# One order table for five engines, exchanged for another: masks, copies and products placed anew in an attention and gated-unit kernel

## The chip, the cores and the metric

The kernel runs on one core of one Trainium2 chip. The metric is the device time of one execution in microseconds (us), the median of several runs. The engines are TensorE (PE, with its weight loads PEld), VectorE (DVE), ScalarE (ACT), GpSimd (POOL) and SyncE (SP), which here only issues DMAs.

## What is computed

Eight batches of 576 rows, eight heads of 64. Attention with a causal mask and a decay from a running sum of `s`; its output `x` goes into a gated linear unit whose gate is a causal convolution of five taps over the rows.

```python
scores = (q @ k.T) / 8 + minimum(cum[k] - cum[q], 0)   # cum = cumsum(max(s, 0)); later keys are masked
x      = softmax(scores) @ v                           # heads side by side: 8 x 576 x 512
gate   = sigmoid(sum(conv_w[j] * x shifted by 4 - j))  # five taps, per column
out    = (gate * (x @ w_val)) @ w_out
```

## The kernel before

The unit of work is a pair of heads of one batch, numbered `n = 4 * batch + pair`, 0 to 31. Its attention gives 128 columns of `x`, and the gated unit then works on those columns, so the same `n` is also a column block of the second half.

**One pair, step by step.** `s0`, `s1`, `s2` are score products on TensorE into two PSUM banks each (L505); `e0`, `e1`, `e2` take their exponentials on ScalarE, 128x1024 elements each, into a buffer `P` (L556; three buffers in turn). The last 64 queries of all four pairs of a batch have their own step, `s4` and `e4` (L532). In `s0` lie the four diagonal blocks, which need the causal mask. It is made in one of two ways: TensorE adds a product of two constant tiles `fut` to the scores, very negative above the diagonal (L518, two products of 512 columns), or GpSimd sets the upper part of `P` to zero after the exponential (`mk`, `AFFINE_SELECT`, L579). The kernel takes the second way for the pairs that have an `mk` step in the table. `av0` and `av` multiply `P` with `Vp` (L594), where `Vp` is `v` times the decay weight, made on GpSimd (`vp`, L474, one instruction per pair). `rec` and `nm` (L607, L613, VectorE) divide by the row sum into `xn`; `xt` turns it (L626, TensorE, into a bank) and `xe` copies the bank to `xT` (L373).

**The gate.** `t1` to `t4` add the four shifted taps into `gp`. On VectorE a tap is one instruction that reads the bank (L665, L670). On GpSimd it is two: `p2`, `p3` or `p4` makes the product `pr` from `xT` (L654), and `t` adds it (L673). ScalarE can make `pr` too (L652). `th` is the tanh (L690), `val` the product with `w_val` (L703), `glu` joins them (L712), `out` is the product with `w_out` (L723), `oe` copies its bank into `ot` (L373), `st` stores it.

**Loads.** Of batches 1 to 7, `q` and `k` come in as fp32 (`ld_q`, `ld_k`), are cast (`c_q`, `c_k`), turned on TensorE (`qq`, L629) and copied into `QKT` (`qe`). `ld_t`, `tt` and `te` do the same for the last 64 rows, `ld_v` loads `v` into `vst`. Nearly all loads and all stores are issued by SyncE, in the order of the table.

**What sets the order.** A table, `ORDER`, a string of 1157 steps. A step is `name.numbers:engine:slots`: `vp.1.0:G` is the decay weighting for pair 0 of batch 1 on GpSimd, `e0.5:A` the first exponential of pair 5 on ScalarE, `s0.4:T:6+7:0` a product into PSUM banks 6 and 7 whose exponentials go into `P` buffer 0. Letters are S (SyncE), G (GpSimd), T (TensorE), A (ScalarE), V (VectorE). The program walks the table once and calls each step's function; every engine gets its instructions in that order, and a framework adds the waits. The last four pairs (batch 7) are cut into rows 0 to 383 and 384 to 575: `u0` to `u3`, `f0` to `f3`, `ml` and steps that end in `.0` or `.1`. `wu` (L620) are products of the identity with itself whose result nobody reads.

Of the kernel before, what the change touches and what calls it, by code (L numbers as in the profile page):

```python
# [197 lines left out]
centre:V s0.1:T:4+5:1 ld_k.1.0:S:2 s2.1:T:2+3 e0.1:A qt.0.2.q:T:1 c_k.0.2:V decT:T:0 ld_cw:S e2.0:A qt.0.2.k:T:4
mk.1:G wu.20:T:5 ld_k.1.1:S qe.0.2.k:V wu.21:T:5 wu.22:T:5 qe.0.2.q:A s1.1:T:6+7 c_k.0.3:V e2.1:A s0.2:T:4+5:2
c_q.0.3:G ld_v.0.2:S expw:A qt.0.3.q:T:1 e1.1:A s4.0.1:T:2+3 qe.0.3.q:V vp.0.0:G qt.0.3.k:T:0 qe.0.3.k:V e4.0.1:A  # L200
ld_q.1.0:S:3 e0.2:A s2.2:T:6+7 s1.2:T:2+3 vp.0.1:G av0.0:T:0+1 e2.2:A av.0:T ld_v.0.3:S mk.2:G rec.0:V av0.1:T:4+5
e1.2:A nm.0:V av.1:T c_k.1.0:G:2 s0.3:T:6+7:0 rec.1:V s2.3:T:2+3 e0.3:A nm.1:V ld_t.1:S cwT:T:0 xt.0:T:1 c_k.1.1:G
cwc:V xt.1:T:4 e2.3:A wu.23:T:6 xe.0:V ld_q.1.1:S vp.0.2:G qq.1.1:T:0:7 t1.0:V:0 s4.0.2:T:2+3 s1.3:T:5+6 e4.0.2:A
xe.1:V c_q.1.0:A:0 s4.0.3:T:2+3 mk.3:G t3.0:V ld_v.1.2:S e4.0.3:A t1.1:V:1 e1.3:A ld_v.1.1:S av0.2:T:2+3 vp.0.3:G
av.2:T t2.0:V ld_v.1.0:S qe.1.3:A tt.1:T:5 ld_v.1.3:S qe.1.2:V p4.1:G:0 p4.0:A:1 ld_v.1.4:S ld_wv:S:4 av0.3:T:6+7
av.3:T te.1:A rec.2:V ld_t.2:S t4.1:G c_q.1.1:G nm.2:V s0.6:T:0+1:1 rec.3:V xt.2:T:5 nm.3:V e0.6:A t4.0:G s0.7:T:2+3:2
xe.2:V s2.6:T:6+7 e0.7:A qq.1.0:T:0:1 t1.2:V:2 mk.6:G p2.1:A:0 s1.6:T:2+3 t3.2:V qe.1.0:A ld_q.2:S:0 mk.7:G qe.1.1:V
e2.6:A t3.1:V s1.4:T:0+1 e1.6:A s0.4:T:6+7:0 t2.2:V ld_k.2:S:1 xt.3:T:4 e0.4:A s0.5:T:2+3:0 t2.1:G t4.2:V s2.4:T:6+7
xe.3:V wu.24:T:5 e2.4:A vp.1.0:G mk.4:G wu.25:T:5 t1.3:V:3 wu.26:T:5 wu.27:T:5 ld_wo:S:2 wu.28:T:5 e1.4:A s4.1.3:T:6+7
ld_t.3:S t3.3:V wu.29:T:5 wu.30:T:5 e4.1.3:A s1.5:T:0+1 t4.3:V wu.31:T:5 th.2:A:0 ld_q.3:S:3 vp.1.2:G av0.4:T:6+7  # L210
th.1:A:1 av.4:T t2.3:V e0.5:A vp.1.1:G cast_wv:G rec.4:V av0.6:T:4+5 nm.4:V av.6:T e1.5:A s2.5:T:2+3 rec.6:V
s1.7:T:6+7 nm.6:V e2.5:A xt.4:T:0 ld_v.2.2:S c_q.2:G:1 tt.2:T:1 xe.4:V th.0:A:2 av0.5:T:2+3 t1.4:V:2 av.5:T te.2:A
ld_v.2.4:S val.3.0:T:4 th.3:A:3 p4.4:G:1 rec.5:V val.3.1:T:1 nm.5:V e1.7:A val.1.0:T:5 glu.3.0:V t4.4:G xt.5:T:2
c_k.2:A:2 glu.3.1:V ld_v.2.1:S val.1.1:T:3 glu.1.0:V s2.7:T:6+7 glu.1.1:V qq.2.0:T:1:5 vp.1.3:G xe.5:V val.0.0:T:3
t2.4:V e2.7:A val.0.1:T:4 t1.5:V:1 p2.5:G:0 qe.2.0:A av0.7:T:6+7 glu.0.0:V glu.0.1:V ld_v.2.3:S val.2.0:T:3 t2.5:G
p3.5:A:1 t3.4:V av.7:T ld_v.2.0:S qe.2.1:A qq.2.1:T:4:2 ld_k.5:S:4 rec.7:V cast_wo:G nm.7:V val.2.1:T:0 qe.2.3:A
xt.6:T:5 glu.2.0:V xt.7:T:1 xe.6:V qe.2.2:A s0.9:T:6+7:1 glu.2.1:V s1.9:T:2+3 p4.5:G:0 xe.7:V out.0.2:T:0 e0.9:A
t1.6:V:0 out.0.0:T:4 t3.5:G t1.7:V:3 e1.9:A ld_k.3:S:0 t4.6:V s1.8:T:6+7 oe.0.2:A:0 s0.8:T:2+3:0 mk.9:G oe.0.0:A:1
t3.7:V val.7.0:T:0 e0.8:A ld_t.4:S out.0.3:T:4 t2.6:V p3.6:G:1 e1.8:A t2.7:V out.0.1:T:2 t3.6:G th.4:A:4 t4.7:V
val.4.0:T:3 st.0.2:S val.7.1:T:7 glu.4.0:V th.7:A:3 val.4.1:T:1 t4.5:G oe.0.3:V:2 th.6:A:1 ld_v.3.2:S s2.8:T:5+6  # L220
glu.7.1:V s4.2.3:T:3+4 glu.7.0:V e2.8:A val.6.0:T:7 glu.4.1:V vp.2.0:G val.6.1:T:0 glu.6.0:V e4.2.3:A ld_v.3.3:S
oe.0.1:V:3 s0.10:T:5+6:2 th.5:A:2 c_q.3:G:0 s2.9:T:3+4 glu.6.1:V av0.8:T:1+2 e2.9:A av.8:T val.5.0:T:0 ld_q.5:S:1
e0.10:A rec.8:V nm.8:V vp.2.1:G s2.10:T:3+4 val.5.1:T:7 e2.10:A glu.5.0:V s1.10:T:1+2 glu.5.1:V s0.11:T:5+6:0 vp.2.2:G
e1.10:A xt.8:T:0 av0.9:T:3+4 xe.8:V tt.3:T:7 e0.11:A p4.8:G:1 t1.8:V:2 av.9:T ld_t.5:S qq.3.0:T:1:2 te.3:A rec.9:V
c_k.3:G:1 nm.9:V s1.11:T:5+6 qe.3.1:A out.0.7:T:7 ld_v.3.4:S t2.8:V qe.3.0:A av0.10:T:3+4 st.0.1:S oe.0.7:V:4 xt.9:T:0
t4.8:G av.10:T e1.11:A xe.9:V ld_v.3.0:S s0.12:T:1+2:1 rec.10:V t1.9:V:3 out.0.6:T:7 e0.12:A vp.2.3:G nm.10:V
ld_v.3.1:S s1.12:T:5+6 oe.0.6:A:5 s2.11:T:1+2 t3.9:V xt.10:T:3 e1.12:A p3.8:G:0 out.0.8:T:7 xe.10:V e2.11:A t4.9:V
ld_q.4:S:2 mk.11:G s2.12:T:5+6 oe.0.8:V:0 e2.12:A qq.3.1:T:4:1 t3.8:G t1.10:V:0 tt.4:T:7 qe.3.3:A av0.11:T:5+6 t2.10:V
st.0.6:S av.11:T p3.10:G:1 qe.3.2:A ld_k.4:S:3 out.0.4:T:1 rec.11:V t4.10:V te.4:A c_q.5:G:2 nm.11:V s0.14:T:3+4:2
st.0.3:S out.0.5:T:7 e0.14:A oe.0.4:V:3 t2.9:V s4.3.3:T:5+6 th.8:A:0 ld_v.4.2:S t3.10:G xt.11:T:4 e4.3.3:A  # L230
s0.13:T:2+3:0 xe.11:V s2.13:T:0+1 e0.13:A ld_v.4.1:S val.8.0:T:5 t1.11:V:1 vp.3.3:G val.10.0:T:6 th.10:A:3 glu.8.0:V
s1.13:T:2+3 t3.11:V vp.3.1:G val.8.1:T:5 e2.13:A st.0.4:S glu.10.0:V t2.11:V e1.13:A val.10.1:T:6 mk.13:G val.9.0:T:0
glu.8.1:V oe.0.5:A:5 ld_k.6:S:0 glu.10.1:V val.9.1:T:1 mk.14:G t4.11:V th.9:A:4 s2.14:T:2+3 qq.5.0:T:7:6 e2.14:A
glu.9.0:V c_k.5:G:0 av0.13:T:4+5 qe.5.0:V av.13:T qe.5.1:A val.11.0:T:0 ld_v.4.4:S rec.13:V glu.9.1:V th.11:A:1
s1.14:T:2+3 s0.15:T:6+7:0 nm.13:V vp.3.2:G e1.14:A val.11.1:T:1 glu.11.0:V xt.13:T:4 ld_v.4.0:S glu.11.1:V e0.15:A
mk.12:G s1.15:T:2+3 xe.13:V s2.15:T:0+1 st.0.5:S t1.13:V:2 e2.15:A qq.5.1:T:7:6 c_q.4:G:1 out.1.1:T:5 t2.13:V qe.5.2:A
qe.5.3:V av0.14:T:0+1 e1.15:A c_k.4:G:2 av.14:T out.1.2:T:7 rec.14:V p4.13:A:0 nm.14:V oe.1.1:A:2 qq.4.0:T:6:2
# [602 lines left out]
```

## Time and profile before

| | |
|---|---|
| median of 3 runs (lowest, highest) | 188.84 us (188.75, 188.96) |
| span of the profiled execution, first to last instruction | 187.6 us |
| busy share: PE, DVE, ACT, POOL | 91%, 87%, 91%, 88% |
| instructions: PE, DVE, ACT, POOL | 2704, 321, 230, 149 |
| HBM read and written | 30.57 MB, 9.44 MB |

No time of the profiled execution is listed beside its span; the median of the runs lies 1.24 us above it. A row of a view by groups reads: line, engine, operation, output <- input with shapes, count | busy us, mean ns of one | idle us of the engine ahead of it and what ended that. A row of the timeline starts with start and length in us. In the table by windows each engine has its busy us and its count. A busy TensorE is not TensorE at its peak, since the ends of products are modelled.

### The profile page before, as it was taken

The numbers are of one execution on the slowest core, as the hardware profiler recorded it, in microseconds if no ns is written. First come the engines' busy times: TensorE is split into PE (matmuls) and PEld (weight loads), VectorE is DVE, ScalarE is ACT, GpSimd is POOL, SyncE is SP. The second block draws the span as 40 slices with busy tenths as digits, with TensorE's granted clock in tenths as the row PEclk, the third lists the DMA queues.
The fourth block names the chain that finished last, engine by engine and source line by source line (L and its number), as shares of the span: only waits on it lengthen the run. The fifth ranks groups of instructions, "written<-read, shape, count | busy, mean of one in ns | idle before, by whom it ended". The sixth has DMA issues, their size and how long they took to land.

```text
span 187.6 us, 6637 instructions
## 1 busy us (share of the span) xinstructions
PE 170.1 (91%) x2704; PEld 113.5 (60%) x2720; DVE 163.3 (87%) x321; ACT 170.6 (91%) x230; POOL 164.5 (88%) x149
## 2 busy tenths in 40 slices
PE   6898885888899998998978999999999999999991
PEld 2556573476757765576745667586566865776560
DVE  4355999878997899999999899998989899999980
ACT  2589899899999999999999999999999999999772
POOL 5267999899999999999978999999999989899610
PEclk9999999999999999999999999999999999999999
DMA  5998999999999999999298999899541003401164
GB/s 164 274 277 246 231 225 243 343 388 341 193 232 304 277 303 258 389 270 283 71 248 184 274 333 325 193 314 247 164 162 66 3 0 115 171 3 56 61 224 175
DMA packets 62283, 40.46 MB, mean 216 GB/s; under 512 B 47333, under 2 KB 49381, under 8 KB 62250
## 3 DMA queue, kind: packets, MB, share of 16 engines
q1 hardware_dynamic: 61706, 39.49, 77.1%
q8 instruction: 22, 0.36, 0.8%
q10 hardware_dynamic: 544, 0.52, 0.8%
q14 instruction: 11, 0.09, 0.2%
HBM read 30.57 MB, written 9.44 MB: 213 GB/s over the span
## 4 chain that ended last, share of the span: by engine, by line
PE 50%; ACT 15%; SPq 9%; DMA 8%; issue 6%; POOL 5%; DVE 4%; ACTq 0%; POOLq 0%; DVEq 0%
PE bank L723 14%; PE bank L703 11%; PE bank L594 10%; ACT P L556 9%; PE bank L505 7%; DMA vst<-in_v_dram 6%; SPq L435 3%; PE bank L629 3%; PE bank L626 3%; POOL gp L673 2%; DMA first<-in_k_dram 2%; ACT th L690 2%; SPq L471 2%; ACT QKT L373 2%; SPq L467 2%
## 5 line engine op out<-in xcount | busy, mean ns | idle before, releaser
L556 ACT ACTIVATE P<-bank 128x1024 bf16<-128x1024 f32 x84 | 82.9, 1042 | 4.1 <-PE bank L505 3.0
L670 DVE SCALAR_TENSOR_TENSOR gp<-bank,cwr,gp 128x574 f32<-128x574 bf16 (+6 forms) x72 | 52.3, 740 | 0.9 <-POOL gp L673 0.5
L673 POOL TENSOR_TENSOR gp<-gp,pr 128x572 f32<-128x572 f32 (+6 forms) x36 | 45.1, 1259 | 4.4 <-DVE gp L670 1.7
L474 POOL TENSOR_TENSOR Vp<-vst,w 128x650 bf16<-128x650 f32 x32 | 40.7, 1288 | 2.8 <-DMA vst<-in_v_dram 1.8
L505 PE MATMUL bank<-QKT 64*128 64x128 bf16 (+4 forms) x592 | 37.2, 237 | 4.8 <-ACT P L556 1.8
L703 PE MATMUL bank<-xT,wv 128*128 128x288 bf16 (+2 forms) x256 | 38.5, 287 | 1.1 <-ACT P L556 0.5
L594 PE MATMUL bank<-Vp,P 128*128 128x65 bf16 x960 | 36.0, 194 | 2.4 <-POOL Vp L474 1.1
L594 PEld LDWEIGHTS <-P 128*128 128x128 bf16 x960 | 33.2, 97 | 6.8 <-issue 1.5
L723 PE MATMUL bank<-wo,glu 128*128 128x512 bf16 x128 | 34.1, 380 | 1.5 <-issue 0.5
L505 PEld LDWEIGHTS <-QKT 64*128 64x128 bf16 x592 | 19.4, 94 | 22.3 <-issue 14.6
L712 DVE SCALAR_TENSOR_TENSOR glu<-th,bank 128x288 bf16<-128x288 f32 (+2 forms) x64 | 27.5, 445 | 2.0 <-ACT th L690 0.9
L703 PEld LDWEIGHTS <-wv 128*128 128x128 bf16 x256 | 22.4, 97 | 11.0 <-issue 4.8
L654 POOL TENSOR_TENSOR pr<-xT,cwr 128x572 f32<-128x572 bf16 (+6 forms) x28 | 28.3, 1020 | 0.6 <-ACT xT L373 0.6
L373 ACT COPY QKT<-bank 128x1024 bf16<-128x1024 bf16 (+1 forms) x26 | 24.2, 966 | 3.8 <-PE bank L489 2.9
L613 DVE TENSOR_TENSOR xn<-bank,recs 128x640 bf16<-128x640 f32 (+2 forms) x36 | 26.8, 745 | 0.6
L665 DVE SCALAR_TENSOR_TENSOR gp<-xT,cwr,bank 128x576 f32<-128x576 bf16 (+2 forms) x36 | 26.4, 741 | 0.7
L579 POOL TENSOR_SCALAR_AFFINE_SELECT P<-P 128x1024 bf16<-128x1024 bf16 (+1 forms) x22 | 22.3, 1021 | 4.2 <-ACT P L556 4.2
L690 ACT ACTIVATE th<-gp,cwr 128x576 f32<-128x576 f32 x28 | 22.0, 794 | 0.1
L723 PEld LDWEIGHTS <-glu 128*128 128x128 bf16 x144 | 12.4, 98 | 13.2 <-issue 1.6
L373 ACT COPY ot<-bank 128x512 f32<-128x512 f32 x26 | 15.2, 610 | 1.5 <-PE bank L723 1.0
L626 PE MATMUL bank<-ident,xn 128*128 128x128 bf16 x164 | 14.9, 219 | 0.7 <-ACT P L556 0.3
L373 POOL CAST qkb<-qkf 128x2048 bf16<-128x2048 f32 (+1 forms) x9 | 14.4, 1619 | 0.0
(66 smaller groups left out, 174.8 us busy)
## 6 DMA issues: line engine op xcount, KB each, us to landing
out_dram<-ot SPq DMA_DIRECT2D x36, 256.0 KB, 4.3
vst<-in_v_dram SPq DMA_DIRECT2D x28, 256.0 KB, 5.9
first<-in_q_dram SPq DMA_DIRECT2D x6, 512.0 KB, 6.0
first<-in_k_dram SPq DMA_DIRECT2D x6, 512.0 KB, 6.2
qkf<-in_q_dram SPq DMA_DIRECT2D x6, 512.0 KB, 6.7
qkf<-in_k_dram SPq DMA_DIRECT2D x6, 512.0 KB, 7.3
vst<-in_v_dram SPq DMA_DIRECT2D x15, 128.0 KB, 5.4
first<-in_q_dram SPq DMA_DIRECT2D x4, 256.0 KB, 5.3
```

The costliest lines, as they stand in the source:

```text
L373: (act.copy if e is act else e.tensor_copy)(dst, src)
L474: e.tensor_tensor(Vps[b % 2][:, :, HP[p]], vslot(b)[:, :, HP[p]], w[:, :, b * 8 + 2 * p:b * 8 + 2 * p + 2].unsqueeze(3).to_broadcast([128, ...
L505: pe.matmul(ps[:, hh, c0:c0 + nq], QKTs[b % 2][r, 1, p, k0:k0 + 128], QKTs[b % 2][r, 0, p, q0:q0 + nq], **kw)
L556: act.activation(out=Pt(n)[:, :, step * 512:(step + 1) * 512], in_=pair((f"s{step}", n)), func=AF.Exp, scale=0.125)
L594: pe.matmul(ps[:, o:o + 65], lhsT, Vps[b % 2][:, kb, 2 * p + w, :], start=(kb == 0), stop=(kb == qb))
L613: vec.tensor_tensor(xns[b % 2][:, g, p * 128:(p + 1) * 128].rearrange("t g (w d) -> t w g d", w=2), ps[:, :, :, 0:64], recs[:, n, :, g].un ...
L654: pool.tensor_tensor(pr, xTs[b % 2][:, c, 4 + lo - m:4 + hi - m], r.to_broadcast([128, hi - lo]), ALU.mult)
L670: vec.scalar_tensor_tensor(gp[:, lo:hi], xps(n, *h)[:, lo - m:hi - m], r, gp[:, lo:hi], ALU.mult, ALU.add)
L673: pool.tensor_tensor(gp[:, lo:hi], gp[:, lo:hi], prs[at[f"p{m}", n, *h][0]][:, lo:hi], ALU.add)
L703: pe.matmul(ps, wv[:, dc, c * 128:(c + 1) * 128], xTs[b % 2][:, dc, 4 + lo:4 + hi], start=(dc == 0), stop=(dc == 3))
L712: vec.scalar_tensor_tensor(glu2[:, c, o + lo:o + hi], th[:, lo:hi], 1.0, ps, ALU.add, ALU.mult)
L723: pe.matmul(bank_of(u, i), glu2[:, c, i * 128:i * 128 + 128], wo[:, c, :], start=(c == 0), stop=(c == 3))
```

## The change

`ORDER` is replaced as a whole: 1119 steps in place of 1157, in another sequence, with other engines for some steps and other banks and buffers. By kind of step, before and after:

- masks on GpSimd: `mk` 18 to 2 (pairs 11 and 25), `ml` 4 to 1; the other masks become products with `fut` on TensorE: 32 more of 512 columns and 6 of 128
- `wu` 32 to 10
- tap products `pr`: ScalarE 8 to 0, GpSimd 28 to 39; taps added on GpSimd 36 to 39, on VectorE 72 to 69
- copies into `QKT` (`qe`): ScalarE 26 to 23, VectorE 10 to 13; copies out of the last product (`oe`): ScalarE 26 to 28, VectorE 10 to 8; copies into `xT` (`xe`): ScalarE 12 to 13, VectorE 24 to 23
- casts of `q` and `k`: ScalarE 3 to 1, VectorE 4 to 3, GpSimd 17 to 20
- the number of every other step, and what it computes, stays

Two lines of the table, the start of it before and after, and the edits outside it:

```diff
-ld_k.0.0:A ld_q.0.0:S ld_k.0.1:A wu.0:T:0 ld_t.0:S wu.1:T:7 wu.2:T:0 wu.3:T:7 ld_s:S wu.4:T:0 ld_q.0.1:S wu.5:T:7
+ld_k.0.1:A ld_k.0.0:A ld_q.0.0:S ld_t.0:S ld_s:S ld_q.0.1:S ld_cw:S ld_q.0.2:S c_k.0.0:V ld_k.0.2:S c_q.0.0:V wu.0:T:7
...
-    Pt = lambda n, h=None: Ps[at["s0" if h is None else f"u{2 * h}", n][1]]
+    split = lambda n: n in splits
+
+    def Pt(n, h=None):
+        steps = ("e0", "e1", "e2") if h is None else (f"f{2 * h}", f"f{2 * h + 1}")
+        return Ps[next(at[f, n] for f in steps if (f, n) in at)[0]]
...
-            split = ("u0", n) in at
-            g = ((3, 1)[h] if split else 4)
-            d = Pt(n, h if split else None)[:, :, 0:128 * g].rearrange("k w (g q) -> k w g q", g=g)
+            g = ((3, 1)[h] if split(n) else 4)
+            d = Pt(n, h if split(n) else None)[:, :, 0:128 * g].rearrange("k w (g q) -> k w g q", g=g)
...
-        two = at["val", n, 0][0]
-        j = two[hf] if isinstance(two, list) else at["val", n, hf][0]
+        j = at["val", n, hf][0]
...
+    splits = {int(name.split(".")[1]) for name, *_ in steps if name.startswith("u0.")}
```

The edits outside the table let the `P` buffer be named on the exponential step (`e0.5:A:0`) and let the three exponentials of a pair come in any order.

**GpSimd around the first `Vp` of batch 1.** These are its rows before, `P` being the buffers of exponentials, `pr` and `gp` tap products and sums, `vst` the loaded `v`:

```order
L654 TENSOR_TENSOR pr_134<-xT_113,cwr 128x572
L673 TENSOR_TENSOR gp_120<-gp_120,pr_134 128x572
L373 CAST qkb_102<-qkf_137 128x2x8x64
L673 TENSOR_TENSOR gp_119<-gp_119,pr_135 128x572
L579 AFFINE_SELECT P_117<-P_117 128x2x512
L579 AFFINE_SELECT P_118<-P_118 128x2x512
L673 TENSOR_TENSOR gp_120<-gp_120,pr_134 128x574
L474 TENSOR_TENSOR Vp_110<-vst_93,w 128x5x130
L579 AFFINE_SELECT P_116<-P_116 128x2x512
L474 TENSOR_TENSOR Vp_110<-vst_93,w 128x5x130 x2
L373 CAST wv<-qkf_138 128x2048
```

The same place on GpSimd in the changed kernel, with the same names:

```order
L657 TENSOR_TENSOR pr_135<-xT_113,cwr 128x574
L373 CAST qkb_103<-qkf_137 128x2x8x64 x2
L676 TENSOR_TENSOR gp_120<-gp_120,pr_134 128x573
L657 TENSOR_TENSOR pr_134<-xT_113,cwr 128x572
L676 TENSOR_TENSOR gp_119<-gp_119,pr_134 128x572
L474 TENSOR_TENSOR Vp_110<-vst_93,w 128x5x130 x3
L676 TENSOR_TENSOR gp_120<-gp_120,pr_135 128x574
L373 CAST wv<-qkf_138 128x2048
```

The two masks ahead of the first `Vp` of batch 1 and the one right behind it are gone, and three `Vp` stand in a row.

**ScalarE about a batch later.** These are its rows before, where the four copies into `QKT` of batch 2 stand; `qkb` is the cast `q` and `k`, `ot` the buffers that are stored:

```order
L373 CAST qkb_104<-first 128x4x8x64
L556 ACTIVATE P_118<-bank 128x2x512
L373 COPY QKT_107<-bank 128x2x2x256
L652 ACTIVATE pr_135<-bank,cwr 128x573
L373 COPY QKT_107<-bank 128x2x2x256 x3
L556 ACTIVATE P_117<-bank 128x2x512 x2
L373 COPY ot_128<-bank 128x512
```

The same copies on ScalarE in the changed kernel, `th` being the tanh and `xT` the turned output of the attention:

```order
L691 ACTIVATE th_125<-gp_119,cwr 128x576
L691 ACTIVATE th_126<-gp_122,cwr 128x576
L373 COPY xT_114<-bank 128x576
L373 COPY QKT_107<-bank 128x2x2x256 x2
L373 COPY xT_114<-bank 128x576 x2
L560 ACTIVATE P_118<-bank 128x2x512
L373 COPY QKT_107<-bank 128x2x2x256
```

The cast and the tap product `pr` have left ScalarE here, one of the four copies into `QKT` has gone to VectorE, and three copies into `xT` have come.

More of the change, by code (lines that the diff above doesn't have):

```diff
@@ L198 @@
[L198 to L237, printed above, removed]
@@ L294 @@
+oe.3.5:V:0 out.3.7:T outa.3.8:T:0 oe.3.7:V:4 st.3.5:S out.3.8:T chk:V st.3.7:S oe.3.8:A:2 cnt:T:7 cntc:V st.3.8:S
+flag:S
 """
@@ L674, in tap @@
         return f
-    split = lambda n: ("u0", n) in at
     def thof(n):
```

160 lines of the change are left out of this document (99 added, 61 removed).

## The prediction

> **What bounds the kernel now.** I read the busy line of the page first, then the table by windows, then the timelines at the places where the windows change character.
>
> ```profile
> PE 170.1 (91%) x2704; PEld 113.5 (60%) x2720; DVE 163.3 (87%) x321; ACT 170.6 (91%) x230; POOL 164.5 (88%) x149
> 0.00:37.81 37.81, 30.74 (x459) 18.79 (x460) 27.27 (x53) 29.84 (x41) 28.49 (x36) 1.00 0.98 251
> 37.81:175.08 137.27, 130.95 (x2176) 89.74 (x2191) 129.00 (x244) 134.14 (x176) 133.42 (x109) 1.00 0.77 212
> 175.08:182.12 7.04, 6.99 (x66) 4.46 (x65) 6.43 (x21) 5.47 (x14) 2.58 (x6) 1.00 0.37 136
> ```
>
> Four engines are within eight us of each other, so none bounds the whole; the windows (busy us of PE, PEld, DVE, ACT, POOL, then clock, DMA share and GB/s) show three stages. Until 37.81 us every engine idles for 7 to 10.5 us while the DMA share is 0.98: the loads bound. From there to 182.12, where the last `glu` ends, lie 144.31 us: ScalarE is busy for 134.14 + 5.47 = 139.61 of them and waits 4.70; TensorE 137.94, GpSimd 136.00, VectorE 135.43. ScalarE is the tightest, and all are tight.
>
> Where the first stage ends is seen in one row each of GpSimd (two), TensorE and VectorE:
>
> ```profile
> 34.23 1.28 POOL L474 TENSOR_TENSOR Vp<-vst,w 128x650 bf16<-128x650 f32 x1 [0.90 <-DMA vst<-in_v_dram]
> 35.46 1.10 POOL L579 TENSOR_SCALAR_AFFINE_SELECT P<-P 128x1024 bf16<-128x1024 bf16 x1
> 36.61 1.09 PE L594 MATMUL bank<-Vp,P 128*128 128x65 bf16 x30 [0.22 <-POOL P L579]
> 37.81 0.22 DVE L607 RECIPROCAL recs<-bank 128x10 f32<-128x10 f32 x1 [0.72 <-PE bank L594]
> ```
>
> `vp.1.0` waits for the load of `v` of batch 1; then comes a mask, then `av0.4` and `av.4`, then `rec.4`. All of batch 1 passes through here. The end:
>
> ```profile
> 178.97 0.59 POOL L673 TENSOR_TENSOR gp<-gp,pr 128x192 f32<-128x192 f32 x1 [0.46 <-DVE gp L670]
> 181.15 0.46 ACT L684 ACTIVATE th<-gp,cwr 128x192 f32<-128x192 f32 x1 [0.28 <-DVE gp L670]
> 181.77 0.35 DVE L712 SCALAR_TENSOR_TENSOR glu<-th,bank 128x192 bf16<-128x192 f32 x1 [0.40 <-PE bank L703]
> ```
>
> GpSimd is done at 179.56, 2.56 us ahead of the last `glu`. Behind that `glu` stand 5.48 us of last products, copies and stores.
>
> **The start, term one.** The number of DMA issues ahead of the last load of `v` of batch 1 on SyncE is the same in both tables (37), and what they load is the same up to the 10 KB of `conv_w`; so I let `vp.1.0` start at 34.23 again, though GpSimd has six masks less to do ahead of it and would be ready earlier. What goes is the mask between `vp.1.0` and `av0.4`: the `Vp` ends at 35.51 and `av0.4` begins at 36.61. The gain lies between 0 (if the exponentials of pair 4 are the later ones, as they come behind the last casts of `q`) and 36.61 - 35.51 = 1.10. I take **0.5**, the middle.
>
> **The long stage, term two.** Mean durations of one, by form, for what leaves and enters each engine after `rec.4`. ScalarE:
>
> ```profile
> L652 ACT ACTIVATE pr<-bank,cwr 128x572 f32<-128x572 bf16 x4 | 3.2, 789 | 0.0
> L652 ACT ACTIVATE pr<-bank,cwr 128x573 f32<-128x573 bf16 x2 | 1.5, 768 | 0.0
> L652 ACT ACTIVATE pr<-bank,cwr 128x192 f32<-128x192 bf16 x1 | 0.4, 437 | 0.0
> L373 ACT COPY QKT<-bank 128x1024 bf16<-128x1024 bf16 x22 | 21.8, 1034 | 0.7 <-PE bank L629 0.6
> L373 ACT COPY ot<-bank 128x512 f32<-128x512 f32 x26 | 15.2, 610 | 1.5 <-PE bank L723 1.0
> L690 ACT ACTIVATE th<-gp,cwr 128x576 f32<-128x576 f32 x28 | 22.0, 794 | 0.1
> L373 ACT CAST QKT<-bank 128x512 bf16<-128x512 f32 x6 | 3.6, 606 | 0.4 <-PE bank L480 0.4
> L373 ACT COPY xT<-bank 128x576 bf16<-128x576 bf16 x7 | 4.6, 656 | 0.0
> L373 ACT COPY xT<-bank 128x384 bf16<-128x384 bf16 x1 | 0.5, 487 | 0.0
> L373 ACT COPY xT<-bank 128x192 bf16<-128x192 bf16 x4 | 1.3, 317 | 0.4 <-PE bank L626 0.4
> ```
>
> Six products go (3 x 0.789 + 2 x 0.768 + 0.437 = 4.34), three `qe` go (3.10), three `oe` come ahead of the last `glu` (1.83), two `th` (1.59, done earlier in the old order), one `te` (0.61), one whole `xe` (0.66), and two halves of 384 stand for two of 192 (0.34). That is -2.4: 137.2.
>
> VectorE:
>
> ```profile
> L373 DVE COPY QKT<-bank 128x1024 bf16<-128x1024 bf16 x6 | 7.3, 1217 | 0.0
> L373 DVE COPY ot<-bank 128x512 f32<-128x512 f32 x10 | 6.8, 683 | 0.0
> L670 DVE SCALAR_TENSOR_TENSOR gp<-bank,cwr,gp 128x574 f32<-128x574 bf16 x22 | 17.6, 807 | 0.6 <-POOL gp L673 0.5
> L670 DVE SCALAR_TENSOR_TENSOR gp<-bank,cwr,gp 128x382 f32<-128x382 bf16 x3 | 1.8, 600 | 0.0
> L373 DVE CAST QKT<-bank 128x512 bf16<-128x512 f32 x2 | 1.4, 687 | 0.2 <-PE bank L480 0.2
> L373 DVE COPY xT<-bank 128x576 bf16<-128x576 bf16 x21 | 9.5, 452 | 1.1 <-PE bank L626 0.9 <-ACT th L690 0.2
> ```
>
> Three `qe` come (3.65), four `oe` fewer stand ahead of the last `glu` (2.73), one tap more (0.81), two half taps fewer (1.20), one `te` (0.69) and one `xe` (0.45) fewer, and two halves of `xT` shrink by under 0.3 in all. That is -0.9: 134.5.
>
> GpSimd:
>
> ```profile
> L579 POOL TENSOR_SCALAR_AFFINE_SELECT P<-P 128x256 bf16<-128x256 bf16 x4 | 1.7, 426 | 0.0
> L654 POOL TENSOR_TENSOR pr<-xT,cwr 128x572 f32<-128x572 bf16 x9 | 10.3, 1147 | 0.2 <-ACT xT L373 0.2
> L654 POOL TENSOR_TENSOR pr<-xT,cwr 128x380 f32<-128x380 bf16 x3 | 2.4, 824 | 0.0
> L654 POOL TENSOR_TENSOR pr<-xT,cwr 128x192 f32<-128x192 bf16 x3 | 1.5, 512 | 0.4 <-ACT xT L373 0.4
> L673 POOL TENSOR_TENSOR gp<-gp,pr 128x572 f32<-128x572 f32 x13 | 18.3, 1406 | 1.7 <-DVE gp L670 1.3
> L673 POOL TENSOR_TENSOR gp<-gp,pr 128x380 f32<-128x380 f32 x3 | 2.9, 997 | 0.0
> ```
>
> Ten masks go (at 1.10, the row at 35.46) and three small ones (1.28); six products come (6.88), two of 384 (1.65), one of 192 (0.51), two whole taps (2.81) and two of 384 (1.99). That is **+1.6**: 137.6. After the load, GpSimd gains nothing from losing its masks, since it is given ScalarE's tap products.
>
> TensorE:
>
> ```profile
> L518 PE MATMUL bank<-fut,fut 64*128 64x512 bf16 x20 | 3.8, 376 | 0.0
> L518 PE MATMUL bank<-fut,fut 64*128 64x256 bf16 x14 | 1.9, 270 | 0.0
> ```
>
> Twenty more products of 512 at 3.8/20 = 0.19 (busy time, since the two halves of the rows lie over each other) and six of 128 at under 1.9/14 = 0.14: +3.8 and at most +0.8, say 4.4 in all: 142.3. No `wu` stood or stands after `rec.4`.
>
> So the load moves from the tightest engine to the others; the sum over four engines even grows by 2.7. What can shorten the stage is only that GpSimd, at 137.6, is then the tightest of the three engines whose busy time is real. It must be done before the last `glu`: the new table ends with `t3.28.1` on GpSimd, then `th` (0.46), `glu` (0.35) and one more `glu` (0.35), 1.16 together, by the rows of the end. 137.6 + 1.2 = 138.8. With the 4.70 us that the tightest engine waits now, the stage takes 143.5 instead of 144.31: **-0.8**. Bounds: if GpSimd waits only 2.0 (estimate: half of its 3.85 between 37.81 and 175.08), 140.8, -3.5; the upper bound is the rival on TensorE.
>
> **The end, term three.** Behind the last `glu` stand one copy on VectorE with a second behind it and one on ScalarE, in place of two on ScalarE; 0.683 against 0.610 each. I take 0.
>
> Sum: -0.5 - 0.8 = -1.3, a span of 186.3. The 1.24 us between span and median are carried over: 188.84 - 1.3 = **187.5 us**.
>
> **Rivals.** *TensorE takes over (slower).* For it: 142.3 busy us of a stage of 143.5. Against it: its busy time counts the drain of each product. It decides if TensorE cannot idle less than 143.5 - 142.3 = 1.2 us. If it idles 3, the stage is 145.3, +1.0; if as now (6.37), 148.7, +4.4. With the start's -0.5: 189.3 to 192.7, middle 191.0.
>
> *The start runs cold (slower).* TensorE's first rows:
>
> ```profile
> 1.44 3.60 PE L620 MATMUL bank<-ident 128*128 128x512 bf16 x8 [1.44 <-POOL ident masks.py:199]
> 6.58 0.81 PE L620 MATMUL bank<-ident 128*128 128x512 bf16 x3
> 5.00:10.00 5.00, 4.48 (x44) 2.69 (x43) 2.42 (x4) 3.32 (x6) 1.67 (x2) 1.00 1.15 268
> 10.00:15.00 5.00, 4.83 (x53) 2.61 (x52) 3.01 (x7) 4.34 (x7) 3.20 (x4) 1.00 1.16 291
> 15.00:20.00 5.00, 4.12 (x93) 3.33 (x93) 2.91 (x7) 4.67 (x8) 4.13 (x4) 1.00 0.85 246
> ```
>
> The first unread products take 0.45 each, later ones 0.27. Of the 4.48 + 4.83 + 4.12 = 13.4 busy us between 5 and 20, 15 unread products take 15 x 0.27 = 4.1; three stay there. If TensorE stays slow without them, 9.3 us of needed products become 9.3 x 0.45/0.27 = 15.5 in 15 us: between 0.5 (what no longer fits) and 6.2 (if all is on the path), I take 3.4, the middle. It decides if more is lost than the slack to the load at 34.23 hides. It gives 187.5 + 3.4 = 190.9. The granted clock in the rows is 1.00 from the start, so it does not speak here.
>
> [...]
>
> *The change moves work and nothing more (no change).* GpSimd keeps all its present waits of the stage: 144.31 - 136.00 - 2.56 = 5.75. Then 137.6 + 5.75 + 1.16 = 144.5, +0.2, with the start -0.3: 188.5.
>
> **How the numbers follow.** Forecast 0.58, TensorE 0.18, cold start 0.12, no change 0.12. About 0.2% (0.4 us) is what a measurement of this kernel can tell from no change. The range runs from 184.2 (both lower bounds together, 188.84 - 1.1 - 3.5) to 191.0, the middle of the TensorE rival; beyond them I leave under 2 in 10. Faster 0.58, same 0.12, slower 0.30.
>
> **What would show it.** Right: `vp.1.0` near 34.2 with a long wait for the load ahead of it, `rec.4` at 37 to 37.8, GpSimd with the smallest idle time from there on, ScalarE with more idle than 4.7. Wrong: `rec.4` after 38.5 with slow products before it (cold start), or waits of ScalarE and VectorE for banks that TensorE fills late (TensorE), or `v` of batch 1 landing clearly before 33, which would bring a gain that I do not count.

## The result, and the profile after

The changed kernel takes 201.12 us (median of 4 runs, 199.96 to 202.63), the kernel before, run beside it, 188.9 us. The ratio is **1.064, with a 95% interval of 1.058 to 1.071**: slower by 12 us, where 187.5 was forecast and 191.0 was the end of the range. The profiled execution has a span of 200.9 us. Times below are medians without the runs that lie more than 1.5% above the fastest of their kernel, which count as a slower state; every ratio is against runs of the kernel before on the same chip, with its 95% interval.

The busy line of the page after:

```profile
PE 174.2 (87%) x2736; PEld 114.9 (57%) x2736; DVE 166.5 (83%) x317; ACT 164.6 (82%) x220; POOL 163.6 (81%) x147
```

This is the row to read first. The four engines do 668.9 us of work between them, before it was 668.5. So, taken together, the engines got no more work; they wait longer. Four engines in 200.9 us idle for 803.6 - 668.9 = 134.7 us, before for 750.4 - 668.5 = 81.9. The difference, 52.8, is 13.2 us for each engine, and the spans differ by 13.3. All of the loss is waiting.

The two stages of the prediction, in the changed kernel (busy us and counts of PE, PEld, DVE, ACT, POOL, then clock, DMA share, GB/s):

```profile
0.00:37.32 37.32, 28.40 (x447) 17.73 (x449) 25.22 (x52) 26.27 (x34) 25.33 (x33) 0.95 0.97 237
37.32:195.41 158.09, 144.26 (x2289) 96.68 (x2283) 139.54 (x260) 137.75 (x186) 138.25 (x115) 0.98 0.71 195
```

`rec.4` comes at 37.32 and the last `glu` ends at 195.41. The long stage has grown from 144.31 to 158.09 us. GpSimd is busy in it for 138.25 (forecast 137.6) and ScalarE for 137.75 (forecast 137.2): these two sums came close. But GpSimd now idles for 19.8 us and ScalarE for 20.3, where the forecast kept 4.7 for the tightest engine.

Where? Windows of 20 us, first of the kernel before, then of the changed one:

```profile
0.00:40.00 40.00, 32.59 (x502) 20.36 (x503) 29.31 (x57) 32.03 (x43) 30.68 (x37) 1.00 0.99 259
60.00:80.00 20.00, 18.95 (x326) 12.55 (x330) 17.76 (x32) 19.43 (x25) 20.00 (x16) 1.00 1.09 303
80.00:100.00 20.00, 18.09 (x378) 13.12 (x378) 19.55 (x33) 19.35 (x26) 18.41 (x14) 1.00 0.89 214
```

```profile
0.00:40.00 40.00, 30.25 (x485) 18.91 (x485) 27.68 (x56) 28.95 (x37) 28.01 (x35) 0.96 0.96 239
60.00:80.00 20.00, 17.90 (x317) 11.65 (x317) 16.82 (x29) 18.41 (x23) 18.43 (x15) 1.00 1.02 288
80.00:100.00 20.00, 14.83 (x266) 11.32 (x268) 12.52 (x22) 13.84 (x17) 14.55 (x11) 0.84 1.07 270
```

Between 80 and 100 us all four engines fall to 12.5 to 14.8 busy us of 20, while the DMA engines are full (1.07) and move more than before. That stretch alone costs (75.40 - 55.74)/4 = 4.9 us.

The table below goes by work in place of time. It adds up the busy time of the four engines from windows of 2 us, without the unread products (`wu`), of which the kernel before has 10.7 busy us and the changed one 5.0; a row gives, for an amount of work done, when the kernel before had done it, and how far the others lag there (us; below zero they are ahead). Two things make it coarse: the four kernels have 658 to 664 us of this work in all, and a product at half clock counts with its longer time (the median unread one 0.632 us in the changed kernel, 0.379 in the kernel before). It is good to about 1.5 us.

| work of four engines, us | before at | changed | changed, without `v` of batches 2 to 7 | changed, loads sorted (last version) |
|---|---|---|---|---|
| 60 | 24.3 | -0.9 | -0.9 | -1.4 |
| 80 | 29.7 | +1.4 | +0.7 | +0.5 |
| 180 | 57.4 | +1.4 | -0.4 | +0.1 |
| 220 | 67.8 | +3.3 | -0.6 | +3.7 |
| 280 | 83.4 | +3.2 | -0.9 | +3.8 |
| 320 | 93.7 | +8.9 | +1.0 | +4.4 |
| 440 | 125.4 | +9.1 | +1.5 | +4.8 |
| 520 | 145.9 | +11.1 | +1.4 | +4.8 |
| 640 | 177.3 | +11.5 | +2.9 | +6.3 |

The changed kernel loses its time in steps, 2.3 us between 23 and 31 us, 1.9 between 59 and 71, 5.7 between 87 and 103, 2.0 between 135 and 157, and runs about as fast as before in between.

The largest step, read from four engines. First SyncE's own row (start, us of issue), then GpSimd, TensorE and ScalarE:

```profile
77.53 1.28 SPq L471 DMA_DIRECT2D vst<-in_v_dram  x2
78.90 2.13 SPq L458 DMA_DIRECT2D tail<-in_q_dram  x1
81.08 1.95 SPq L458 DMA_DIRECT2D tail<-in_k_dram  x1
83.07 0.78 SPq L471 DMA_DIRECT2D vst<-in_v_dram  x1
83.90 1.07 SPq L435 DMA_DIRECT2D qkf<-in_q_dram  x1
85.02 1.68 SPq L435 DMA_DIRECT2D qkf<-in_k_dram  x1
```

```profile
91.68 3.73 POOL L373 CAST qkb<-qkf 128x2048 bf16<-128x2048 f32 x2 [5.45 <-DMA qkf<-in_k_dram]
```

```profile
93.62 1.03 PE L632 MATMUL bank<-ident,qkb 64*128 64x64 bf16 x32 [4.00 <-POOL qkb L373]
```

```profile
94.70 1.01 ACT L373 COPY QKT<-bank 128x1024 bf16<-128x1024 bf16 x1 [3.80 <-PE bank L632]
```

`ld_k.5`, half of `q` and `k` of batch 5, is issued from 83.90, behind three loads of `v` and one of the tails, one of them `v` of batch 5 itself. It lands at 91.68, the cast waits 5.45 us for it, the turns wait for the cast, the copy for the turns. Every engine takes its instructions in the order of the table (ScalarE's 219 activations, copies and casts stand in the trace in that order), so whatever stands behind these four waits too.

The waits of the changed kernel name the same chain (us in total, times, longest), and the chain that ended last has moved, here before and after:

```profile
ACT QKT L373 <- PE bank L632: 9.2, 4, 3.8
POOL qkb L373 <- DMA qkf<-in_k_dram: 9.1, 3, 5.4
DVE QKT L373 <- PE bank L632: 8.8, 3, 6.0
...
POOL Vp L474 <- DMA vst<-in_v_dram: 3.9, 3, 1.8
POOL Vp L474 <- DMA out_dram<-ot: 3.8, 1, 3.8
```

```profile
PE 50%; ACT 15%; SPq 9%; DMA 8%; issue 6%; POOL 5%; DVE 4%; ACTq 0%; POOLq 0%; DVEq 0%
```

```profile
POOL 25%; SPq 23%; DVE 15%; DMA 14%; issue 10%; ACT 7%; PE 5%; POOLq 0%; DVEq 0%; ACTq 0%
```

Half of the end's chain was TensorE's products; now 37% of it is SyncE issuing and DMAs moving, which were 17%.

### The profile page after: what moved, and what is told of

The parts are those of the page before. It is cut to its first block, busy times and chain, and to the rows that moved or that the text cites. A ratio compares the mean times of both kernels' runs of the same rounds, so it can differ in the third digit from the quotient of the medians.

```text
span 200.9 us, 6682 instructions
## 1 busy us (share of the span) xinstructions
PE 174.2 (87%) x2736; PEld 114.9 (57%) x2736; DVE 166.5 (83%) x317; ACT 164.6 (82%) x220; POOL 163.6 (81%) x147
## 4 chain that ended last, share of the span: by engine, by line
POOL 25%; SPq 23%; DVE 15%; DMA 14%; issue 10%; ACT 7%; PE 5%; POOLq 0%; DVEq 0%; ACTq 0%
POOL gp L676 10%; SPq L471 10%; POOL pr L657 7%; SPq L435 7%; POOL Vp L474 6%; DVE gp L673 4%; DMA out_dram<-ot 4%; ACT P L560 4%; DMA tail<-in_k_dram 3%; DVE glu L712 3%; DMA vst<-in_v_dram 3%; DMA first<-in_q_dram 2%; DVE gp L668 2%; SPq L458 2%; SPq L467 2%
## 5 line engine op out<-in xcount | busy, mean ns | idle before, releaser
L673 DVE SCALAR_TENSOR_TENSOR gp<-bank,cwr,gp 128x574 f32<-128x574 bf16 (+5 forms) x69 | 51.3, 748 | 1.4 <-DVE recs L610 0.2
L676 POOL TENSOR_TENSOR gp<-gp,pr 128x572 f32<-128x572 f32 (+6 forms) x39 | 48.5, 1246 | 2.1 <-DVE gp L673 1.0
L505 PE MATMUL bank<-QKT 64*128 64x128 bf16 (+4 forms) x592 | 38.6, 240 | 3.6 <-ACT P L560 3.3
L657 POOL TENSOR_TENSOR pr<-xT,cwr 128x572 f32<-128x572 bf16 (+6 forms) x39 | 39.5, 1020 | 2.2 <-ACT xT L373 0.6
L723 PE MATMUL bank<-wo,glu 128*128 128x512 bf16 x144 | 36.3, 380 | 0.7 <-POOL wo L373 0.4
L373 ACT COPY QKT<-bank 128x1024 bf16<-128x1024 bf16 (+1 forms) x23 | 21.7, 976 | 12.9 <-PE bank L632 9.2
L712 DVE SCALAR_TENSOR_TENSOR glu<-th,bank 128x288 bf16<-128x288 f32 (+2 forms) x64 | 26.6, 447 | 2.6 <-ACT th L691 1.3
L373 DVE COPY QKT<-bank 128x1024 bf16<-128x1024 bf16 (+1 forms) x13 | 13.2, 1017 | 12.5 <-PE bank L632 8.8
L373 POOL CAST qkb<-first 128x2048 bf16<-128x2048 f32 (+1 forms) x11 | 15.4, 1419 | 7.5 <-DMA first<-in_q_dram 4.5
L723 PEld LDWEIGHTS <-glu 128*128 128x128 bf16 x144 | 12.2, 97 | 14.3 <-issue 2.8
L373 ACT COPY ot<-bank 128x512 f32<-128x512 f32 x28 | 16.1, 604 | 2.5 <-PE bank L723 2.3
```

The lines of the kernel that those rows point to most:

```text
L373: (act.copy if e is act else e.tensor_copy)(dst, src)
L505: pe.matmul(ps[:, hh, c0:c0 + nq], QKTs[b % 2][r, 1, p, k0:k0 + 128], QKTs[b % 2][r, 0, p, q0:q0 + nq], **kw)
L657: pool.tensor_tensor(pr, xTs[b % 2][:, c, 4 + lo - m:4 + hi - m], r.to_broadcast([128, hi - lo]), ALU.mult)
L673: vec.scalar_tensor_tensor(gp[:, lo:hi], xps(n, *h)[:, lo - m:hi - m], r, gp[:, lo:hi], ALU.mult, ALU.add)
L676: pool.tensor_tensor(gp[:, lo:hi], gp[:, lo:hi], prs[at[f"p{m}", n, *h][0]][:, lo:hi], ALU.add)
L712: vec.scalar_tensor_tensor(glu2[:, c, o + lo:o + hi], th[:, lo:hi], 1.0, ps, ALU.add, ALU.mult)
```

## The experiments

The theories at the start. **A**: the loads come too late, because the new order of SyncE puts loads that are needed later ahead of those needed now, while the DMA engines are full. **B**: ten unread products in place of 32 leave TensorE at half its clock in places (the granted clock is 0.50 from 28.75 to 32.16 us and from 93.6 to 100.4 us). **C**: TensorE and GpSimd were given too much work. Two came later. **E**: the DMA engines simply move too little by 110 us for this row of work, in whatever order. **F**: TensorE runs out of loaded code. Kernels called "without `v`" leave out the loads of `v` of the batches named, so that part of `x` is computed from stale data; nothing else in them differs.

**Without the loads of `v`, in both kernels.**

```diff
     def ld_v(e, b, i):
+        if b >= 2:
+            return
         vst = vslot(b)
```

For the changed kernel: 

> The changed kernel without the loads of v of batches 2 to 7 (it computes with those of batches 0 and 1): 7.1 of 30.6 MB less to read, everything else in the same order. Theory A (loads come late because SyncE issues v of batches 3 and 5 ahead of q and k that are needed sooner, while the DMA engines are full): 187 to 191 us, and GpSimd's waits for loads fall from 24 us to under 10. Theory B (TensorE loses its full clock at the start and twice later for want of unread products, and that is the cause): 198 us or more. Theory C (the work given to TensorE and GpSimd is too much): 194 to 198 us.

For the kernel before: 

> The kernel before without the same loads of v of batches 2 to 7. Theory A: 185 to 188.5 us, as only the few waits for loads behind 40 us go (about 1 us for v at 99 us); so the two kernels come within 3 us of each other. Theories B and C: the distance between the two light kernels stays at 8 us or more.

Measured: 192.58 us for the changed one (ratio 1.014, 1.007 to 1.021), 189.33 for the one before (0.999, 0.996 to 1.003). The kernel before hides these loads of `v`; in the changed one they cost 201.1 - 192.6 = **8.5 of the 12.2 us** (9.5 by the ratios). Some 3 us stay.

**More unread products.** Thirty-four more `wu`, in front of the turns of batch 1 and of batch 5 and at the start, where the clock is low.

```diff
 wu.4:T:7
+wu.10:T:7 wu.11:T:7 wu.12:T:7 wu.13:T:6 wu.14:T:6 wu.15:T:6
...
+wu.16:T:5
...
+wu.25:T:5
 qq.1.0:T:5:6
...
+wu.26:T:0
...
+wu.43:T:0
 qq.5.0:T:0:1
```

> The changed kernel with 34 more unread products: 6 at the start, 10 ahead of the first turn of q of batch 1, 18 ahead of the first turn of batch 5, which are the places where the granted clock fell. Theory B: the clock stays at full speed from about 6 us on and the time falls by 4 us or more, to 193 to 197. Theory A: the clock may stay up, but the casts still wait for their loads: 199 to 202 us.

Measured: 203.3 us (1.075, 1.067 to 1.084). The mean clock went from 0.971 to 0.995, and no time came back. The added products take TensorE's time too (12.2 busy us of unread products in place of 5.0), so this shows that more of them do not help, not that the slow clock costs nothing; but it does not look like the 12 us. (Some 2 us of this run's time lie at its end: see the last section.)

**One part alone, in the kernel before.** Three edits of the old table, one for each theory.

```diff
 ld_v.2.0:S
+ld_v.3.2:S ld_v.3.3:S ld_v.3.4:S ld_v.3.0:S ld_v.3.1:S
...
-ld_v.3.2:S
-ld_v.3.3:S
...
-ld_v.3.1:S
```

> The kernel before with nothing moved but the five loads of v of batch 3, up right behind those of batch 2, as the changed table has them in the same stretch. A: the halves of q and k and the stores behind them come later, 3 to 8 us slower than before. C: no change, within 0.5 us of before.

```diff
-mk.0:G
...
-ml.31:G
```

(17 of the 18 whole masks in fact, all but `mk.11`.) 

> The kernel before with nothing changed but the masks: 16 of the 18 whole masks and 3 of the 4 small ones go from GpSimd to TensorE, as in the changed kernel. A: masks are not the cause, within 1 us of before. C: TensorE gets some 4 us of products on top of 170, 2 to 5 us slower than before.

```diff
-wu.10:T:2
...
-wu.31:T:5
```

> The kernel before with the last 22 of its 32 unread products taken out, and nothing else: ten are left, as in the changed kernel. B in part: half clock somewhere between 10 and 34 us and 1 to 2.5 us slower. If they are worth nothing: within 0.5 us of before.

Measured: five loads of `v` moved up, 192.4 us (**1.017, 1.010 to 1.024**); masks on TensorE, 191.7 (**1.015, 1.008 to 1.021**); ten unread products, 190.6 (**1.007, 1.003 to 1.012**). So each part costs something by itself in that kernel: 3.1, 2.7 and 1.4 us by the ratios. In the first the order of five loads is all that differs; SyncE spends 13 us on ten loads of `v` in a row, and nothing else is issued:

```profile
43.44 13.15 SPq L470 DMA_DIRECT2D vst<-in_v_dram  x10
```

The second shows what masks on TensorE do. These are the busy line and the chain:

```profile
PE 175.2 (92%) x2760; PEld 114.2 (60%) x2760; DVE 163.1 (86%) x321; ACT 171.0 (90%) x230; POOL 145.3 (76%) x129
...
PE 60%; SPq 11%; DMA 8%; DVE 7%; ACT 6%; issue 4%; POOL 2%; DVEq 0%; ACTq 0%; POOLq 0%
```

GpSimd gets 19 us freer and TensorE 5.1 us busier, its share of the chain goes from 50% to 60%, and the kernel is slower. It looks as if waits for GpSimd were traded for TensorE's own time. The third run brings the half clock back; its rows between 10 and 20 us show the clock at 0.60 and 0.50, where the kernel before has 1.00:

```profile
10.00:15.00 5.00, 3.54 (x34) 2.14 (x35) 2.90 (x7) 3.85 (x6) 2.58 (x3) 0.60 1.16 297
15.00:20.00 5.00, 5.00 (x71) 3.79 (x68) 1.95 (x5) 4.32 (x7) 4.43 (x4) 0.50 1.02 281
```

**Sorting the loads of the changed kernel, four attempts.** First: all five loads of `v` of batch 3 behind `ld_k.5`, those of batch 5 behind batch 4, `ld_q.4` and `ld_k.5` earlier. The diff shows a stretch of SyncE's row alone; the four `vp` of batch 3 were also put further back on GpSimd, so this run moves more than loads.

```diff
-ld_v.3.1 ld_v.2.2 ld_q.3 ld_v.3.3 ld_v.2.3 ld_v.3.2 ld_v.2.1 ld_v.2.4 ld_v.3.4 ld_v.3.0 ld_q.5 ld_t.3 ld_t.4 ld_k.3 ld_k.4 st.0.3
+ld_v.2.2 ld_q.3 ld_v.2.3 ld_v.2.1 ld_v.2.4 ld_q.5 ld_t.3 ld_t.4 ld_k.3 ld_q.4 ld_k.4 ld_k.5 ld_v.3.1 ld_v.3.3 ld_v.3.2 ld_v.3.4 ld_v.3.0 st.0.3
```

> The changed kernel with its loads in the order of their need: v of batch 3 behind k of batch 5 and not with v of batch 2, v of batch 5 behind v of batch 4, q of batch 4 and k of batch 5 ahead of them; the four weightings of batch 3 go behind the casts that were waiting. All else as in the change. Theory A: 189 to 194 us, the wait of 5.4 us for k of batch 5 is gone. Theory B: 199 us or more, unless the clock stays up too. Theory C: 196 to 200 us.

Measured: 204.5 us (two runs, 203.2 and 205.9; 1.081 of the kernel before). Missed. The waits of this kernel say why:

```profile
ACT ot L372 <- DMA out_dram<-ot: 6.3, 1, 6.3
DVE ot L372 <- ACT ot L372: 5.6, 1, 5.6
PE bank L596 <- ACT ot L372: 5.2, 1, 5.2
...
POOL qkb L372 <- DMA qkf<-in_k_dram: 3.4, 4, 2.0
```

The wait that was aimed at fell from 9.1 to 3.4, but the five loads of `v` now stood ahead of three stores. SyncE's row shows it:

```profile
64.13 10.37 SPq L470 DMA_DIRECT2D vst<-in_v_dram  x5
74.60 1.78 SPq L730 DMA_DIRECT2D out_dram<-ot  x3
```

Issuing them took 10.4 us, the stores began at 74.60, and the copies that need their buffers stood until 78.64. Loads and stores stand in one row here; a load moved back to its need is moved in front of something else.

Second and third: only `ld_k.5` forward, ahead of three loads of `v` and the tail; then also three loads of `v` of batch 3 behind batch 2.

```diff
 ld_q.4:S:2
+ld_k.5:S:3
...
-ld_k.5:S:3
```

> The changed kernel with one step moved: the load of the second half of q and k of batch 5 goes onto SyncE right behind the first half of batch 4, ahead of three loads of v and one of the tails. A (the loss is waits for loads that stand too late in SyncE's row): in the changed kernel all four engines stand still for 4 to 6 us between 88 and 94 us, until GpSimd's cast of that half has its data at 91.68; that stall goes, 196 to 197.5 us. C (too much work on TensorE and GpSimd): the time stays within 1 us of 201.

```diff
-ld_v.3.1:S
...
-ld_v.3.3:S
...
-ld_v.3.2:S
...
 ld_v.2.4:S
+ld_v.3.1:S ld_v.3.3:S ld_v.3.2:S
```

> As the kernel with the earlier load for batch 5, and three loads of v of batch 3 go behind the last load of v of batch 2, so that the four Vp of batch 2 start earlier. A: the stall at 57 to 64 us (1.8 us on all engines) goes as well: 194 to 196 us. C: no change from the other kernel of this pair, both near 201.

Measured: 204.0 us (1.079, 1.070 to 1.087) and 201.8 (1.069, 1.057 to 1.080). Both missed: A's gain does not come, though the 5.45 us wait of that cast is gone from their traces. Within 14 us they stand at the next late things, a stop of TensorE (3.3 and 3.8 us, below) and a load of the tails (3.3 and 3.2 us).

Fourth: the row sorted up to batch 5, `v` of batch 2 ahead of batch 3 and of batch 4 ahead of batch 5, `ld_t.5` ahead of `ld_t.6`, `ld_k.7` behind `ld_k.6`, the last `v` of batch 6 ahead of three stores, the mask of pair 25 on TensorE. Four loads of `v` of batch 6 still stand behind the five of batch 7. First with the 34 unread products, then without.

```diff
-st.0.2 ld_q.4 ld_v.4.4 ld_v.5.0 ld_t.6 ld_v.4.1 ld_k.5 st.0.4 ld_v.4.2 ld_k.7 st.0.5 ld_v.4.3 ld_v.4.0 ld_q.6 st.0.6 ld_t.5
+st.0.2 ld_q.4 ld_k.5 ld_t.5 ld_v.4.4 ld_v.4.1 st.0.4 ld_v.4.2 ld_v.4.3 ld_v.4.0 st.0.5 ld_q.6 ld_v.5.2 ld_v.5.3 st.0.6 ld_t.6
...
-ld_v.6.3 st.1.6 st.1.0 st.1.1 ld_v.6.1
+ld_v.6.3 ld_v.6.1 st.1.6 st.1.0 st.1.1
...
-mk.25:G
```

> The changed kernel with SyncE's row sorted by need: v of batch 2 ahead of batch 3, of batch 4 ahead of batch 5, the half of q and k and the tail of batch 5 ahead of those of batches 6 and 7, the last load of v of batch 6 ahead of three stores; besides 34 more unread products at the three cold places and the whole mask of pair 25 on TensorE. A (loads of the near batches stand behind loads of far ones while the DMA engines are full): the lags at 22 to 30, 57 to 64, 85 to 101, 133 to 139 and 149 to 156 us of the changed kernel (2.1, 1.8, 5.6, 0.9 and 1.2 us of all engines) mostly go: 189 to 194 us. E (the DMA engines move too little up to 110 us in this row of work, whatever stands first): another load is late in place of each, 198 to 204 us.

> The changed kernel with its loads sorted by need and the mask of pair 25 on TensorE, as before, but without the 34 unread products. In the three kernels that had them, 6.1 us pass between the last reduction and the end of the span, with two loads of TensorE's code in them, against 3.6 to 4.1 us and one load in the others. A, with that end taken off: 196 to 198.5 us. If the unread products were worth what they showed at 22 to 30 us (2 us) and the end does not change: 200 to 202.

Measured: 199.9 us (1.051, 1.043 to 1.058) and 199.0 (1.053, 1.047 to 1.059). Sorting by hand brings back about 2 of the 8.5 us that the loads of `v` cost, so A's numbers were missed, in the first of the two E's held, and the second lies between the two that were written down. The 2 us that the unread products seemed to bring back at 22 to 30 us, in the second expectation, were about half they themselves, counted as work: without them it is 1.0 us (the lag at 80 us of work falls from 1.4 to 0.4).

**Order or volume.** Ten loads of `v` left out, the same bytes in both: batches 3 and 5 (which the changed table puts ahead of nearer needs), or 4 and 6.

```diff
     def ld_v(e, b, i):
+        if b in (3, 5):
+            return
         vst = vslot(b)
```

> The changed kernel without its ten loads of v of batches 3 and 5 (those sums come out wrong), which are the ones put ahead of nearer needs. A: most of the 8.5 us that all the loads of v were worth comes back: 193 to 196 us. E: as much as any other ten loads bring, the same as without batches 4 and 6.

> The changed kernel without its ten loads of v of batches 4 and 6, as many bytes as batches 3 and 5. A: only part comes back, 197 to 200 us. E: the same as without batches 3 and 5, within 1.5 us.

Measured: 193.1 us (1.021, 1.011 to 1.032) without 3 and 5, 196.9 (1.035, 1.028 to 1.042) without 4 and 6. They differ by 3.8 us (2.5 by the ratios, whose intervals just overlap), not under 1.5, so which loads they are seems to count (A); but either ten bring 4 to 8 us, and together (8.0 + 4.2) more than leaving out all does, so any relief of the queue helps (E). Both hold in part.

**What stays without `v`.** The 34 unread products, then ten at one place only, then the sorted row, each without the loads of `v` of batches 2 to 7.

```diff
+wu.10:T:5
...
+wu.19:T:5
 qq.1.0:T:5:6
```

All 34: 

> The changed kernel without the loads of v of batches 2 to 7 and with the 34 unread products more. B in part (the half clock at 28 to 32 us costs 2 us, which waits for loads had hidden in the kernel with these products alone): 190 to 191, against 192.6 without them. If B has no part: 192.6 or above.

Ten, as in the diff: 

> The changed kernel without the loads of v of batches 2 to 7, with ten unread products more ahead of the products at 28 us instead of 34 in three places. B in part: the half clock at 28 to 32 us goes and the end stays at one load of code: 190.5 to 191.8 against 192.6. If the unread products are worth nothing: 192.6 or above.

The sorted row: 

> The same with the loads of v of batches 2 to 7 left out (those sums come out wrong). What is left over the kernel before is then neither v nor the order of the other loads. A alone: 189 to 190.5. If the rest sits in the cold start, in TensorE's code loads and in the end: 191.5 to 193, as without the sorting.

Measured: 196.4 us (1.033, 1.022 to 1.044), 193.0 (1.022, 1.014 to 1.030), 192.3 (1.016, 1.009 to 1.022), against 192.6 without any of it. Unread products bring nothing here either, and the order of the other loads is not what stays. In the sorted row the loads of `v` still cost 199.0 - 192.3 = 6.7 us.

**The stop of TensorE.** In the sorted kernel TensorE stands in the middle of five turns of `xn`, with no releaser:

```profile
93.23 0.64 PE L631 MATMUL bank<-ident,qkb 64*128 64x64 bf16 x32
93.81 0.34 PE L628 MATMUL bank<-ident,xn 128*128 128x128 bf16 x3
97.06 0.29 PE L628 MATMUL bank<-ident,xn 128*128 128x128 bf16 x2 [2.91 <-issue]
```

The changed kernel without `v` has the same stop at the same place:

```profile
88.44 0.64 PE L634 MATMUL bank<-ident,qkb 64*128 64x64 bf16 x32
89.02 0.34 PE L631 MATMUL bank<-ident,xn 128*128 128x128 bf16 x3
92.02 0.28 PE L631 MATMUL bank<-ident,xn 128*128 128x128 bf16 x2 [2.66 <-issue]
```

The kernel that differs from this one by ten more unread products far ahead of it, and by nothing else:

```profile
90.97 0.55 PE L634 MATMUL bank<-ident,qkb 64*128 64x64 bf16 x25
93.84 0.29 PE L634 MATMUL bank<-ident,qkb 64*128 64x64 bf16 x7 [2.32 <-issue]
94.06 0.45 PE L631 MATMUL bank<-ident,xn 128*128 128x128 bf16 x5
```

The stop came behind the 32nd turn and three more; now it comes behind the 25th, exactly ten products earlier in the row. A wait for data would have stayed with its product. So it is tied to the position in TensorE's code, as F has it; that the code came late there was not shown. The trace of the changed kernel itself has no such stop; there the cast of `ld_k.5` holds TensorE at this place. The last two runs move 32 of the turns ahead of that place to behind three groups of scores, so that TensorE does not pass them and the products around them at one stretch.

```diff
-qq.4.1:T:3:5
...
-qe.4.2:A
...
-qe.4.3:V
...
 oe.1.1:V:2
+qq.4.1:T:3:5 qe.4.2:A qe.4.3:V
```

> The changed kernel with its loads sorted by need and the mask of pair 25 on TensorE, and the last 32 of the turns of batch 4, with their two copies, moved behind three groups of scores, so that TensorE does not go through four blocks of turns and two pairs of the product with Vp at one stretch. F (TensorE runs through its code faster there than the code is loaded, and stands for 2.9 us in the middle of a group): the stop goes, 196 to 197 us against 199.0. If the stop was something else or another takes its place: 198.5 or above.

> The same without the loads of v of batches 2 to 7 (those sums come out wrong). F: 189.5 to 190.5 against 192.3, so that a step of 2.7 us at 90 to 97 us is explained. If not: 192 or above.

Measured: 197.0 us (1.046, 1.037 to 1.055) and 192.1 (1.019, 1.012 to 1.025). The stop shrinks to 0.33 and, in the second kernel, 0.66 us, and stands between two products with `Vp`:

```profile
91.56 0.39 PE L598 MATMUL bank<-Vp,P 128*128 128x65 bf16 x7
92.60 0.42 PE L598 MATMUL bank<-Vp,P 128*128 128x65 bf16 x8 [0.66 <-issue]
```

With all loads it brought 2.0 us, as F had it (1.4 by the ratios, whose intervals overlap); without `v` nothing, since waits of 0.7 to 1.1 us on several engines stand in its place. The stop is real, but taking it away does not bring the rest back. 197.0 us is the best version of the changed table; none beats the kernel before.

## Why the prediction was wrong

*The start, -0.5: the number right, in part by luck.* `vp.1.0` was to come at 34.2 with a wait for its load, `rec.4` at 37 to 37.8:

```profile
33.87 3.76 POOL L474 TENSOR_TENSOR Vp<-vst,w 128x650 bf16<-128x650 f32 x3 [0.77 <-DMA vst<-in_v_dram]
```

```profile
37.32 0.22 DVE L610 RECIPROCAL recs<-bank 128x10 f32<-128x10 f32 x1 [0.74 <-PE bank L597]
```

37.81 became 37.32. But 0.36 of these 0.49 us come from the load, which lands earlier (33.87 in place of 34.23), a gain that was not counted. From the end of the first `Vp` to `av0.4` it is 0.97 us now and was 1.10: the mask is gone, but TensorE then waits for exponentials of ScalarE (the condition that the prediction names for a gain of 0):

```profile
35.62 0.40 PE L505 MATMUL bank<-QKT 64*128 64x64 bf16 x4 [0.51 <-ACT P L560]
36.12 1.09 PE L597 MATMUL bank<-Vp,P 128*128 128x65 bf16 x30
```

And `rec.4` was a poor milestone: by work done the changed kernel was already 1.3 us behind there, since other steps had been put back. Of the signs of being right, `rec.4` at 37 to 37.8 and a ScalarE that idles for more than 4.7 us both came, so they did not tell a gain from a loss of 12 us; GpSimd's idle time was not the smallest (19.8 us, TensorE 13.8, VectorE 18.6).

*The long stage, -0.8: wrong, and here is the failed step.* The busy times came out within 1 us on ScalarE and GpSimd, on GpSimd with some luck: the kernel before has eleven whole masks after `rec.4` and the changed one two, so nine go and not ten. With nine, the sum is 138.7 (measured 138.25) and the stage 144.6 in place of 144.31, so the forecast would have been about no change. VectorE was busy for 139.5 us, where 134.5 was forecast. But a miscount of 1.1 us is not the loss. What failed is the half sentence "With the 4.70 us that the tightest engine waits now". The waits were carried over from the old order into one in which every load had another place. The prediction counts SyncE's issues only up to `v` of batch 1 and does not follow its row further, though the DMA share of the long stage stood in the quoted row (0.77), and windows of 5 us of the kernel before show 0.99 to 1.22 from 25 to 90 us. The runs put in its place: the waits of the tightest engine are 19.8 us and not 4.7; the loads of `v` cost 0 us before and 8.5 us after (shown by leaving them out); moving five of them alone costs 3.1 us in the kernel before (shown); and the cast of `ld_k.5` that stood 5.45 us is only the first in the queue, since removing its wait alone gained nothing (shown).

*TensorE takes over: its mechanism is real, its place another.* With the masks alone the kernel before gets 2.7 us slower, inside the +1.0 to +4.4 us that this rival was priced at for its stage. In the changed kernel TensorE idles for 13.8 us of the long stage, twice the 6.4 of before, so it does not bound it.

*The start runs cold: real, and smaller than priced.* 1.4 us in the kernel before, against 3.4. The granted clock, of which the prediction says that it "does not speak here", reads 0.60 and 0.50 there once the products are gone. The changed kernel is slow at its start too, where its clock column reads 1.00: there is no clock record in its trace before 11.7 us (before: 6.4), but its unread products (shortest, median and longest in ns) take as long there as the two at 31 us, where the clock is 0.50. First the kernel before, then the changed one:

```profile
L620 PE MATMUL bank<-ident x32: 376/379/634, 1.4 to 36.0; 128*128 128x512 bf16 x32
```

```profile
L623 PE MATMUL bank<-ident x10: 606/632/634, 1.4 to 31.7; 128*128 128x512 bf16 x10
```

Yet at 60 us of work it is not behind. It is 1.4 us behind at 31 us, of which 1.0 came back with more unread products and was lost again by 49 us.

*The end, 0: right.* Behind the last `glu` stand 5.5 us, as before. Ahead of it, in the long stage, GpSimd's taps now hold the last tanhs; ScalarE's waits for them, up to 187.11 and 189.08 us, are 0.80 and 1.35 us.

*What stays open.* Of 12.2 us, 8.5 are tied to the loads of `v`, but sorting and spreading brought back only 4.1, so how much of the 8.5 is order and how much volume is not settled; no run has the loads of batches 6 and 7 in order. At 100 us both kernels have moved the same 26.3 to 26.4 MB (their windows of GB/s added up), the changed one with 31 us less work of its four engines done: it is not short of bytes by then, but of those that it needs. Of the other 3 to 4 us, the cold start (1.4) and the masks (2.7) would make up the sum if they cost in the changed kernel what they cost in the old one; that was not shown. The table by work points elsewhere: without `v` the changed kernel is not behind at 83 us and 1.9 us further back at 94, and in between its trace has the stop of TensorE. But spreading the turns took that stop down to 0.66 us and gained nothing, so this stays open too.
